# Single-bank evictions for batch 0: mix units that leave PSUM by two engines side by side, and turns and last DFTs that rotate over all eight banks

## The chip, the cores and the metric

The kernel runs on one core of a Trainium2 chip. The metric is the device time of one execution in microseconds (us). The kernel before takes 849.84 us (median of three executions, 849.62 to 851.12). One trace per kernel was taken by the hardware profiler. Engines are named as in the profile: PE is TensorE (matmuls), DVE is VectorE, ACT is ScalarE, POOL is GpSimd, SP issues transfers. PSUM, where matmuls write, is used here as eight banks of 512 float32 columns for each of 128 partitions; the pools below take them all.

## The reference

A frequency-domain mixer is followed by a feed-forward layer. Cut to what matters:

```python
# x: 8 batches x 3008 positions x 256 channels, float32
X = np.fft.rfft(x, axis=1)
Yr = Xr @ w_r - Xi @ w_i + b_r          # 256 x 256, complex
Yi = Xr @ w_i + Xi @ w_r + b_i
Yr = np.sign(Yr) * np.maximum(np.abs(Yr) - 0.01, 0.0)      # likewise Yi
y = np.fft.irfft(Yr + 1j * Yi, n=3008, axis=1)
# feed-forward on 24064 tokens, hidden width 2048
g = s * np.maximum(y @ w_in, 0.0) ** 2 + b
out = g @ w_out
```

## The kernel before

The transforms of length 3008 = 94 x 32 are done as matmuls. Batch 0 runs alone at the front, as nothing is there yet to lie beside it; the batches 1 to 7 are mixed into the feed-forward matmuls of the batch before, and there PE is full. Only batch 0 is changed. Its path, in six *units* for each half of the output channels (`ec`):

first DFT -> `mix` (96 matmuls) -> copy g out of PSUM -> `fwd_dft` -> soft threshold (Relu on ACT into m, then z on DVE) -> `inv_dft` -> copy vt -> `turn` (a transpose by the identity) -> copy vs -> `last_dft` -> copy yt -> feed-forward.

The bias must be added once. DVE adds it while it copies g; ACT here only copies, so where it does, a *seed* matmul puts the bias into the bank of the forward DFT first.

```python
hpool = ...tile_pool(name="psh", bufs=2, PSUM)   # two tiles of two banks
apool = ...tile_pool(name="psa", bufs=2, PSUM)   # two single banks
fpool = ...tile_pool(name="psf", bufs=2, PSUM)   # two single banks
def evac(dst, src, cols): ...   # ACT or DVE, whichever has the lower sum of estimates

def mix(ec, u):
    ps = two_banks().rearrange("p h (j r e) -> p (h j) r e", j=2, r=2)
    for j in range(4):
        ...                                   # 2 matmuls of 256 columns for each j
    g = vpool.tile([P, 4, 2, P], F16, ...)
    if u % 3 == 1:
        nc.scalar.copy(out=g, in_=ps)         # 1,024 columns, bias by a seed
    else:
        nc.vector.tensor_tensor(out=g, in0=ps, in1=b_g[...], op=ALU.add)

def fwd_dft(ec, u):
    seeded = u % 3 == 1
    if seeded:
        nc.tensor.matmul(ps, sel_t, b_h[...], start=True, stop=False, ...)
    for j in range(4):
        ...                                   # 2 matmuls of 128 columns for each j
    # Relu on ACT, then z on DVE

def turn(ec, k):
    ps = two_banks()
    ...                                       # 8 matmuls
    evac(vs[...], ps[0:96]..., 1024)

def last_dft(ec, n2):
    ps = [one_bank(), other_bank()]
    ...                                       # 8 matmuls, two evac of 384

# the loop over the twelve units
    mix(*steps[i]); fwd_dft(*steps[i - 1]); inv_dft(*steps[i - 2])
    k = i - U - 2
    if 0 <= k < 4:
        turn(0, k)
    if 0 <= k - 1 < 4:
        last_dft(0, 8 * (k - 1))
    if i >= 2 * U:
        some(3)                               # three pieces of batch 1's first DFT
# then, for the second half: turn(1, k), some(1), last_dft(1, 8 * (k - 1))
```

## Time and profile before

| | before |
|---|---|
| span of the trace | 847.2 us |
| PE busy | 833.7 us, 98% |
| DVE, ACT busy | 691.5 us, 641.2 us |
| first mix starts | 13.72 us |
| batch 1's first forward DFT starts | 64.58 us |

What the change takes apart is seen in the groups by shape, here of the kernel before between 13.7 and 50 us. A row has the line, engine, operation and tiles, output and input shape, the count, then the busy time in us and the mean ns of one, then the idle time before them with what ended it:

```profile
L419 DVE TENSOR_TENSOR g<-psh,b_g 128x1024 f16<-128x1024 f32 x8 | 9.7, 1217 | 0.6 <-PE psh L409 0.5
...
L171 ACT CAST vs<-psh 96x1024 f16<-96x1024 f32 x6 | 6.1, 1012 | 0.7 <-PE psh L473 0.6
L416 ACT CAST g<-psh 128x1024 f16<-128x1024 f32 x4 | 4.1, 1014 | 0.1
L175 DVE CAST vs<-psh 96x1024 f16<-96x1024 f32 x2 | 2.4, 1215 | 0.2 <-PE psh L473 0.2
```

All twelve copies g and all eight copies vs are of 1,024 columns, and take 1.0 us on ACT or 1.2 on DVE. Whatever else is queued on that engine stands behind such a copy, and both of the tile's banks stay taken until it is done.

### The profile page before, as it was taken

How to read it: one execution, taken by the hardware profiler on the slowest of the kernel's cores; microseconds unless marked ns; L12 is line 12 of the kernel's file. 1: busy time of each engine (PE TensorE's matmuls, PEld its weight loads, DVE VectorE, ACT ScalarE, POOL GpSimd, SP SyncE). 2: the span in 40 equal slices, each digit the busy share in tenths (PEclk: the TensorE clock that was granted, in tenths of full speed). 3: DMA queues.
4: the chain of work that ended last, by engine and by line, in shares of the span. 5: the costliest groups of instructions: out<-in, count | busy, mean ns of one | idle time of the engine just before them, and what ended most of it. 6: DMA issues, size and time to landing. Idle time of an engine off the chain costs nothing.

```text
span 847.2 us, 17072 instructions
## 1 busy us (share of the span) xinstructions
PE 833.7 (98%) x6645; PEld 598.8 (71%) x6645; DVE 691.5 (82%) x1016; ACT 641.2 (76%) x854; POOL 45.6 (5%) x71
## 2 busy tenths in 40 slices
PE   7999999999999999999999999999999999999997
PEld 6757767777677766777677776777667777766765
DVE  5899987888878987888878888798977888776674
ACT  5888877787778877787777887787877777766673
POOL 4331000000000000000000000000000000000000
PEclk9999999999999999999999999999999999999999
DMA  8946467224762367324762248613354223411111
GB/s 200 173 131 139 118 160 192 78 70 108 193 161 60 99 157 191 95 79 108 179 173 57 73 105 202 170 41 91 101 156 120 61 79 98 112 33 39 38 44 50
DMA packets 105746, 96.06 MB, mean 113 GB/s; under 512 B 9542, under 2 KB 97482, under 8 KB 104322
## 3 DMA queue, kind: packets, MB, share of 16 engines
q1 hardware_dynamic: 99218, 80.55, 32.9%
q0 software_dynamic: 6448, 14.42, 10.5%
q8 instruction: 52, 0.85, 0.4%
q14 instruction: 28, 0.23, 0.1%
HBM read 53.52 MB, written 46.66 MB: 118 GB/s over the span
## 4 chain that ended last, share of the span: by engine, by line
PE 87%; DVE 4%; ACT 3%; DMA 3%; issue 2%; SPq 0%; POOL 0%; DVEq 0%; ACTq 0%; POOLq 0%
PE psa L819 36%; PE psh L748 35%; PE psf L614 4%; PE psf L549 2%; PE psf L600 2%; PE psf L585 2%; PE psf L644 2%; PE psf L697 2%; ACT rt L755 1%; DVE gt L762 1%; DMA out_dram<-ost 1%; DMA x<-in_x_dram 1%; DMA us<-ud 1%; DMA F_c<-dft_fwd 1%; PE psh L409 1%
## 5 line engine op out<-in xcount | busy, mean ns | idle before, releaser
L755 ACT ACTIVATE rt<-psh 128x1024 f32<-128x1024 f32 (+2 forms) x384 | 386.9, 1009 | 119.3 <-PE psh L748 117.9
L762 DVE TENSOR_TENSOR gt<-rt 128x1024 f16<-128x1024 f32 (+2 forms) x321 | 384.1, 1200 | 97.9 <-ACT rt L755 97.2
L819 PE MATMUL psa<-w_out_t,gt 128*128 128x256 f16 (+1 forms) x3024 | 454.3, 272 | 0.1
L819 PEld LDWEIGHTS <-gt 128*128 128x128 f16 (+1 forms) x3024 | 301.0, 101 | 187.2 <-issue 1.7
L748 PE MATMUL psh<-yt,w_in 128*128 128x512 f16 (+1 forms) x1344 | 396.7, 378 | 0.3 <-ACT rt L755 0.3
L748 PEld LDWEIGHTS <-w_in 128*128 128x128 f16 x1536 | 142.9, 98 | 27.4 <-issue 2.1
L829 DVE SCALAR_TENSOR_TENSOR ost<-psa,s_bc,bias_bc 128x512 f32<-128x512 f32 (+2 forms) x97 | 71.1, 733 | 8.3 <-PE psa L819 7.1
L759 ACT ACTIVATE gt<-rt 128x1024 f16<-128x1024 f32 (+2 forms) x63 | 66.2, 1051 | 1.0
L619 DVE TENSOR_TENSOR ring<-psf,s 128x512 f16<-128x512 f32 x84 | 57.6, 685 | 3.7 <-PE psf L614 3.1
L171 ACT CAST v<-psf 128x512 f16<-128x512 f32 x78 | 45.2, 581 | 18.8 <-PE psf L644 18.8
L171 ACT CAST xf<-psf 128x512 f16<-128x512 f32 x82 | 47.9, 585 | 10.9 <-PE psf L585 10.9
L171 ACT CAST u<-psf 96x512 f16<-96x512 f32 x77 | 44.6, 580 | 11.0 <-PE psf L549 10.7
L748 PE MATMUL psh<-tail,w_in 128*128 128x512 f16 (+1 forms) x192 | 52.1, 353 | 0.0
L614 PE MATMUL psf<-W_g,xf 128*128 128x256 f16 x336 | 50.4, 273 | 0.0
L171 ACT CAST yt<-psf 128x480 f16<-128x480 f32 (+2 forms) x75 | 38.1, 521 | 13.6 <-PE psf L697 13.6
L200 POOL DMA_DIRECT2D x<-in_x_dram x36 | 18.7, 526 | 429.7 <-PE psf L549 428.6
L549 PE MATMUL psf<-x,A_t 94*96 94x512 f16 x104 | 39.7, 381 | 1.7 <-ACT yt L171 0.5
L625 DVE TENSOR_TENSOR ring<-ring,high 128x512 f16<-128x512 f16 x84 | 35.5, 423 | 2.3
L626 DVE TENSOR_TENSOR ring<-ring 128x512 f16<-128x512 f16 x84 | 35.5, 423 | 1.9
L624 DVE TENSOR_TENSOR ring<-ring,low 128x512 f16<-128x512 f16 x84 | 35.4, 422 | 1.6
L614 PEld LDWEIGHTS <-xf 128*128 128x128 f16 x336 | 32.9, 98 | 3.8
L697 PE MATMUL psf<-C_t,vs 96*128 96x96 f16 x448 | 33.0, 205 | 0.1
(88 smaller groups left out, 489.4 us busy)
## 6 DMA issues: line engine op xcount, KB each, us to landing
out_dram<-ost SPq DMA_DIRECT2D x152, 128.0 KB
ud<-u SPq DMA_DIRECT2D x28, 384.0 KB
us<-ud SPq DMA_DIRECT2D x28, 384.0 KB
vd<-v SPq DMA_DIRECT2D x42, 256.0 KB
vs<-vd SPq DMA_DIRECT2D x14, 768.0 KB
x<-in_x_dram POOLq DMA_DIRECT2D x28, 376.0 KB, 6.8
ring<-ring SPq DMA_DIRECT2D x280, 32.0 KB
out_dram<-ost SPq DMA_DIRECT2D x16, 120.0 KB
```

Of the source, the lines that this page charges most:

```text
L171: return None, nc.scalar.copy(out=dst, in_=src)
L549: nc.tensor.matmul(ps[0:96, :], A_t[0:N1, :], x16[(b, c)][0:N1, j * D : (j + 2) * D], start=True, stop=True,)
L614: nc.tensor.matmul(ps[:, r, :], xt[:, 2 - r, dc], W_g[:, dc, r], start=(dc == 0), stop=(dc == DC - 1),)
L619: nc.vector.tensor_tensor(out=t, in0=ps, in1=hold[i // 2][:, i % 2].unsqueeze(1).to_broadcast([P, 2, D]), op=ALU.add,)
L625: nc.vector.tensor_tensor(out=m, in0=m, in1=high, op=ALU.min)
L697: nc.tensor.matmul(ps[:, j * 96 : (j + 1) * 96], vs[(b, h)][:, k, ec * P : (ec + 1) * P], C_t, start=True, stop=True,)
L748: nc.tensor.matmul(o, w_in_t[dc][:, mc * P : (mc + 1) * P], r, start=(dc == 0), stop=(dc == DC - 1),)
L755: nc.scalar.activation(out=rt[:, :, 0:w], in_=ps[:, :, 0:w], func=AF.Relu)
L759: nc.scalar.activation(out=gt[:, :, 0:w], in_=rt[:, :, 0:w], func=AF.Square)
L762: nc.vector.tensor_tensor(out=gt[:, :, 0:w], in0=rt[:, :, 0:w], in1=rt[:, :, 0:w], op=ALU.mult)
L819: nc.tensor.matmul(ps[0:size, h, :], gts[(ti, mc // 2)][:, mc % 2, sub * size : (sub + 1) * size], w_out_t[:, mc, :], start=(mc == 0), sto ...
L829: nc.vector.scalar_tensor_tensor(out=ost[0:size, 0:k], in0=ps[0:size, 0:k], scalar=s_bc[0:size], in1=bias_bc[0:size, 0:k], op0=ALU.mult, o ...
```

## The change

The intent: while batch 0 runs, the four banks of `psh` are a pool of single banks, `psm`. A mix unit fills two of them; DVE empties one half and ACT the other, side by side. Turns are cut in halves as well. Turns, last DFTs and batch 1's first DFT take a bank from all eight in rotation, and the last DFTs of the first half are moved behind the forward DFT of the last unit. The pool `psm` is closed after batch 0, and `psh` opens in its place.

```diff
+    def any_bank():
+        turn_of[0] += 1
+        if "h" in pools:
+            return (other_bank, one_bank)[turn_of[0] % 2]()
+        return (mix_bank, one_bank, mix_bank, other_bank)[turn_of[0] % 4]()
... in mix
-            ps = two_banks().rearrange("p h (j r e) -> p (h j) r e", j=2, r=2)
+            for half in range(2):
+                ps = mix_bank().rearrange("p (j r e) -> p j r e", j=2, r=2)
...
-            if u % 3 == 1:
-                nc.scalar.copy(out=g, in_=ps)
+                if half:
+                    nc.scalar.copy(out=g[:, 2:4], in_=ps)
+                else:
+                    nc.vector.tensor_tensor(out=g[:, 0:2], in0=ps, in1=b_g..., op=ALU.add)
... in fwd_dft: every unit is seeded, for its second half alone
-            if seeded:
-                nc.tensor.matmul(ps, sel_t, b_h...[P, 4, P] ...)
+                if j == 2:
+                    nc.tensor.matmul(ps[:, 2:4], sel_t, b_h...[P, 2, P] ...)
... in turn
-            ps = two_banks()
-            for j in range(8):
+            for i in range(2):
+                ps = any_bank() if ec else mix_bank()
+                for j in range(4):
... in last_dft
+            if ec or n2 >= 16:
+                ps = [any_bank(), any_bank()]
+            else:
+                ps = [one_bank(), other_bank()]
... in the loop
-            if 0 <= k - 1 < 4:
-                last_dft(0, 8 * (k - 1))
+            for n in {1: (0,), 2: (8,), 4: (16, 24)}.get(k, ()):
+                last_dft(0, n)
... in batch 1's first DFT
-            ps = other_bank() if more_banks and i % 2 else one_bank()
+            ps = any_bank() if more_banks else one_bank()
... at the end of the program's front
-    more = first_batch()
+    with tc.tile_pool(name="psm", bufs=4, space=PSUM) as pool:
+        pools["m"] = pool
+        more = first_batch()
+    pools["h"] = ctx.enter_context(tc.tile_pool(name="psh", bufs=2, space=PSUM))
```

More of the change, by code (lines that the diff above doesn't have):

```diff
@@ L145 @@
     bigpool = ctx.enter_context(tc.tile_pool(name="big", bufs=1))
-    hpool = ctx.enter_context(tc.tile_pool(name="psh", bufs=2, space=bass.MemoryType.PSUM))
     apool = ctx.enter_context(tc.tile_pool(name="psa", bufs=2, space=bass.MemoryType.PSUM))
@@ L176, in evac, with mix_bank @@
         return nc.vector.tensor_scalar_mul(out=dst, in0=src, scalar1=scale), None
+    pools = {}
+    def mix_bank():
+        return pools["m"].tile([P, 512], F32, name="psm", tag="psm")
+    turn_of = [0]
+    def any_bank():
[3 more added lines that the diff above has]
+        return (mix_bank, one_bank, mix_bank, other_bank)[turn_of[0] % 4]()
     def two_banks():
-        return hpool.tile([P, 2, 512], F32, name="psh", tag="psh")
+        return pools["h"].tile([P, 2, 512], F32, name="psh", tag="psh")
     def one_bank():
@@ L356, in first_batch @@
             for dc in range(DC):
-                ps = one_bank() if dc else two_banks()[:, 0]
+                ps = one_bank() if dc else mix_bank()
                 with tc.issue_after(last_pe.ins):
@@ L404, in mix @@
         def mix(ec, u):
-            ps = two_banks().rearrange("p h (j r e) -> p (h j) r e", j=2, r=2)
-            for j in range(4):
-                q = 4 * u + j
-                for dc in range(DC):
-                    nc.tensor.matmul(
-                        ps[:, j], ut[:, dc, 4 * q : 4 * q + 4, :],
-                        W_t[:, dc, :, ec * P : (ec + 1) * P],
-                        start=(dc == 0), stop=(dc == DC - 1),
-                    )
-            g = vpool.tile([P, 4, 2, P], F16, name="g0", tag="v")
-            if u % 3 == 1:
-                nc.scalar.copy(out=g, in_=ps)
-                load["act"] += 1.02
-            else:
-                nc.vector.tensor_tensor(
-                    out=g, in0=ps,
-                    in1=b_g[:, :, ec * P : (ec + 1) * P].unsqueeze(1).to_broadcast([P, 4, 2, P]),
-                    op=ALU.add,
-                )
-                load["dve"] += 1.2
-            gs[(ec, u)] = g
+            g = vpool.tile([P, 4, 2, P], F16, name="g0", tag="v")
+            gs[(ec, u)] = g
+            for half in range(2):
+                ps = mix_bank().rearrange("p (j r e) -> p j r e", j=2, r=2)
+                for j in range(2):
+                    q = 4 * u + 2 * half + j
+                    for dc in range(DC):
+                        nc.tensor.matmul(
+                            ps[:, j], ut[:, dc, 4 * q : 4 * q + 4, :],
+                            W_t[:, dc, :, ec * P : (ec + 1) * P],
+                            start=(dc == 0), stop=(dc == DC - 1),
+                        )
+                if half:
+                    nc.scalar.copy(out=g[:, 2:4], in_=ps)
+                    load["act"] += 0.58
+                else:
+                    nc.vector.tensor_tensor(
+                        out=g[:, 0:2], in0=ps,
+                        in1=b_g[:, :, ec * P : (ec + 1) * P].unsqueeze(1).to_broadcast(
+                            [P, 2, 2, P]
+                        ),
+                        op=ALU.add,
+                    )
+                    load["dve"] += 0.69
         def fwd_dft(ec, u):
@@ L429, in fwd_dft @@
             g = gs.pop((ec, u))
-            seeded = u % 3 == 1
-            if seeded:
-                nc.tensor.matmul(
-                    ps, sel_t,
-                    b_h[:, ec * P : (ec + 1) * P].unsqueeze(1).to_broadcast([P, 4, P]),
-                    start=True, stop=False, skip_group_check=True,
-                )
             for j in range(4):
                 q = 4 * u + j
+                if j == 2:
+                    nc.tensor.matmul(
+                        ps[:, 2:4], sel_t,
+                        b_h[:, ec * P : (ec + 1) * P].unsqueeze(1).to_broadcast([P, 2, P]),
+                        start=True, stop=False, skip_group_check=True,
+                    )
                 for r, f in enumerate((F_t[:, q, :], F_2[q // H][:, q % H, :])):
                     nc.tensor.matmul(
-                        ps[:, j, :], f, g[:, j, r, :], start=(r == 0 and not seeded),
-                        stop=(r == 1), skip_group_check=seeded,
+                        ps[:, j, :], f, g[:, j, r, :], start=(r == 0 and j < 2),
+                        stop=(r == 1), skip_group_check=True,
                     )
@@ L470, in turn @@
         def turn(ec, k):
-            ps = two_banks()
-            for j in range(8):
-                nc.tensor.matmul(
-                    ps[0:96, j // 4, (j % 4) * P : (j % 4) * P + P],
-                    vt[:, ec, 8 * k + j, :], eye_t, start=True, stop=True,
-                )
-            h, n = divmod(8 * k, HW)
-            evac(
-                vs[(0, h)][:, n : n + 8, ec * P : (ec + 1) * P],
-                ps[0:96].rearrange("p h (j e) -> p (h j) e", e=P), 1024,
-            )
+            for i in range(2):
+                ps = any_bank() if ec else mix_bank()
+                n = 8 * k + 4 * i
+                for j in range(4):
+                    nc.tensor.matmul(
+                        ps[0:96, j * P : j * P + P], vt[:, ec, n + j, :], eye_t,
+                        start=True, stop=True,
+                    )
+                h, n = divmod(n, HW)
+                evac(
+                    vs[(0, h)][:, n : n + 4, ec * P : (ec + 1) * P],
+                    ps[0:96].rearrange("p (j e) -> p j e", e=P), 512,
+                )
         yt = yts[0] = ypool.tile([P, DC, N2, 96], F16, name="yt", tag="yt")
         def last_dft(ec, n2):
-            ps = [one_bank(), other_bank()]
+            if ec or n2 >= 16:
+                ps = [any_bank(), any_bank()]
+            else:
+                ps = [one_bank(), other_bank()]
             for j in range(8):
@@ L844, in schedule @@
             plan.setdefault(start + (i * span) // len(units), []).append(u)
-    more = first_batch()
+    with tc.tile_pool(name="psm", bufs=4, space=bass.MemoryType.PSUM) as pool:
+        pools["m"] = pool
+        more = first_batch()
+    pools["h"] = ctx.enter_context(
+        tc.tile_pool(name="psh", bufs=2, space=bass.MemoryType.PSUM)
+    )
     load.update(act=0.0, dve=0.0)
```

## The prediction

> **What bounds the kernel now.** I read the page's busy slices first, then the windows of the first 58 us, then the waits of TensorE, then its timeline. TensorE (PE) is busy 98% of the span, and the slices show where the rest is:
>
> ```profile
> PE   7999999999999999999999999999999999999997
> ```
>
> Only the first and the last slice (21 us each) fall below nine tenths. The change touches batch 0 alone, which is the front of the program, so the windows there matter:
>
> ```profile
> core 0: us, PE busy (x) PEld busy (x) DVE busy (x) ACT busy (x) POOL busy (x), PEclk, DMA share, GB/s
> ...
> 13.70:35.00 21.30, 19.68 (x238) 16.84 (x239) 15.97 (x24) 16.96 (x25) 8.70 (x13) 1.00 0.95 215
> 35.00:42.00 7.00, 5.54 (x74) 4.38 (x72) 6.54 (x10) 5.80 (x12) 1.75 (x3) 1.00 0.91 126
> 42.00:50.00 8.00, 7.13 (x84) 4.80 (x82) 7.07 (x12) 6.96 (x13) 7.50 (x7) 1.00 0.34 100
> 50.00:58.00 8.00, 7.71 (x38) 3.62 (x37) 7.20 (x8) 8.00 (x12) 0.73 (x1) 1.00 0.33 98
> ```
>
> From 35 us on VectorE (DVE) and ScalarE (ACT) are nearly full while PE has holes: the emptying of PSUM bounds it. From 50 to 58 ACT has no idle time at all. Before 35 PE looks full, but a matmul's record is longer than its place in the queue, so I count starts instead. In the timeline:
>
> ```profile
> 16.77 0.22 PE L440 MATMUL psf<-g,F_t 128*128 128x128 f16 x1 [1.09 <-DVE g L419]
> 16.82 0.22 PE L440 MATMUL psf<-g,F 128*128 128x128 f16 x1
> ...
> 17.21 1.04 PE L409 MATMUL psh<-W_t,ut 128*128 128x256 f16 x8
> 18.08 0.38 PE L432 MATMUL psf<-b_h,sel_t 128*128 128x512 f16 x1
> 18.30 0.22 PE L440 MATMUL psf<-g,F_t 128*128 128x128 f16 x1
> ```
>
> The start-to-start times are 0.055 us for a matmul of 128 columns, 0.109 for 256 (0.87 for eight), 0.216 for 512 (18.08 to 18.30), and likewise 0.042 for 96. The same reading of the DVE and ACT timelines gives their pitch: DVE 1.13 us for 1,024 columns of PSUM, 0.60 for 512, 0.46 for 384; ACT 0.91, 0.48 and 0.38, with 0.58 for the Relu of 512.
>
> Work of PE from 13.72 (first mix) to 61.53, the point from which the instruction order of the two kernels is identical to the end: 96 mix matmuls x 0.109 = 10.4; 96 forward x 0.055 = 5.3; 4 seeds 0.9; 48 inverse 2.7; 64 turns 3.5; 64 last DFTs 2.7; 16 of batch 1's first DFT x 0.216 = 3.5; 42 of the first feed-forward matmul 9.1; 16 of the second 1.7; bias 0.1. Sum 39.9 of 47.8 us. So 7.9 us is all that could be won, under 1% of 849.84; after 61.5 PE is dense (119.63 busy of 120 from 80 to 200).
>
> **What the Trainium skill says.** "Perfetto Trace Analysis", section "Optimizing Scalar/DVE Operations", gives about 125 ns per-instruction overhead for DVE on PSUM and 51 ns for Scalar on PSUM, and says that where they cause bubbles on other engines, "breaking up instructions may allow work to be completed sooner". The trace: two halves cost 2 x 0.60 - 1.13 = 0.07 us more on DVE and 2 x 0.48 - 0.91 = 0.05 on ACT, so DVE pays less here than the page says. The same page, "Matmul Optimizations", asks that all 8 PSUM banks be used; before, the turns use only the two double tiles (psh), the last DFTs only psf and psa. "TensorE: Matmul & The Clock Gate", section "Wait — 56ns, not 53.3ns?", gives 55.6 and 215.7 ns start to start at 128 and 512 columns; the trace agrees.
>
> **The change, part by part.**
> Mix. Before, 8 of 12 units leave by DVE (8 x 1.13) and 4 by ACT (4 x 0.91), 12.7 us. After, 12 x 0.60 on DVE and 12 x 0.48 on ACT, 13.0: DVE loses 1.8, ACT gains 2.1, so the automatic balance sends more later copies to DVE. PE gets 12 seeds of 256 columns for 4 of 512: 12 x 0.109 - 4 x 0.216 = +0.45 us.
> Turns. 8 x 1,024 columns become 16 x 512: about 8.6 instead of 7.7 us, half on each engine.
>
> I laid the new instruction order out by hand with these pitches, 0.20 us from a matmul group's end to its reader, 0.06 from a copy's end (start plus duration, 0.69 DVE, 0.58 ACT) to PE.
>
> (a) First forward DFT. PE waits 1.09 us for g. The DVE half now ends at 16.15 instead of 16.71, but the ACT half can start only when ACT has placed F_t (16.24) and ends at 16.85, so the second half of the forward group starts at 16.9. Its end moves from 17.21 to 17.1: gain 0.1.
>
> (b) Steady steps. PE per step: mix 0.87 + forward 0.44 + seed 0.11 + inverse 0.22 = 1.64. Before, mix 2 to mix 8 took 17.21 to 27.60, 1.73 per step, because each z queued behind a 1.13 us copy. After, the inverse needs z, which comes 0.20 + 0.69 + 0.03 + 0.69 + 0.06 = 1.7 us after its forward group, while PE has 1.64 of other work: some 0.03 to 0.1 lost per step. Forward group 7 ends at 28.8 instead of 29.36: gain 0.5 in all.
>
> (c) The turns begin. Before, mix 9 waits 0.28 for the double tile behind the turn; after, it does not. Step 10 lies about 1.0 earlier.
>
> (d) The end of the mixes. Before, forward 11 waits for z and inverse 11 comes only after batch 1's DFTs, themselves waiting:
>
> ```profile
> 39.02 0.22 PE L440 MATMUL psf<-g,F_t 128*128 128x128 f16 x1 [0.65 <-DVE z L447]
> ...
> 40.64 0.38 PE L549 MATMUL psa<-x,A_t 94*96 94x512 f16 x1 [0.44 <-DVE vt L175]
> ...
> 43.28 0.38 PE L549 MATMUL psa<-x,A_t 94*96 94x512 f16 x1 [0.31 <-DVE vt L175]
> 43.50 1.06 PE L473 MATMUL psh<-eye_t,vt 128*96 128x128 f16 x16
> ```
>
> After, forward 11 goes before the last DFTs (37.2) and the DFTs take any free bank; the last vt is out at 41.1 and the second half's turns start at 41.2 instead of 43.5. Gain 2.1 to 2.3 here.
>
> (e) The tail. Both evicting engines are full: 9 copies u, 8 vs (512 columns) and 8 yt (384) at a joint rate of 1/0.60 + 1/0.48 = 3.75 and 1/0.46 + 1/0.38 = 4.8 per us is 4.5 + 1.7 = 6.2 us, ending at 47.4 plus small waits. The feed-forward tiles (psh) now take over the banks of batch 0 and cannot be interleaved with the last DFTs as before (first one at 47.45); PE reaches them at 47.6, and ACT's first rt is at 48.65 instead of 49.97. Then 1 copy u is left instead of 4 (3 of them on ACT, about 1 us).
>
> (f) To the common order ACT bounds: nine rt x 0.95, one u 0.5, two bias copies 0.4 each after 48.65: 58.6, the common matmul at 59.0 instead of 61.3. VectorE's squares run back to back from 49.7 and are 2.0 earlier.
>
> Sum of what each part adds: (a) 0.1, (b) 0.4 more, (c) 0.5 more, (d) 1.2 more, and (e) and (f) hold it at 61.3 - 59.0, about 2.2 us, with the 0.45 us of seeds already inside. All of it lies on PE's path, as PE is dense afterwards. I take 2.1: 847.7 us.
>
> **The rivals.**
> *The gain is given back at the hand-over.* The psh tiles wait for the last batch 0 copy, PE and ACT start the feed-forward cold. For: the pool of four banks closes before they open. Against: by (e) the last of those copies is out at about the same 47.5. If each of the last copies slips by half a microsecond the gain is 1 us: 848.8.
> *ACT becomes the bound in the steps.* It gets 2.1 us more, and its Relu must wait behind a g half. Per step ACT has 0.48 + 0.58 + 0.48 = 1.54 with every vt on it, under PE's 1.64, so only queueing hurts; if each of twelve steps lost 0.15, 1.8 us go, and the time is about 849.5.
> *A transfer holds it.* GpSimd's w_sum, behind the load of w_out (landed at 41.4), is ready at 50.8, and PE meets it after sixteen feed-forward matmuls, by my layout at 51.6. That is a floor 0.8 us below: 847 at best. Other loads (w_in, x of batch 1) land ten microseconds before use.
> *Better packing than by hand.* If PE's holes shrank to 4 us, 846.5, less the floor just named.
>
> **Range and chances.** The ceiling of 7.9 us and the worst rival, a full undoing with the seeds on top (850.5), lie well within 2% (17 us). The three runs before spread over 1.5 us. Range 846.4 to 849.3; faster by over 2% 0.01, within 2% 0.98, slower 0.01.
>
> **What would show it.** DVE's g at 0.69 us and ACT's at 0.58, x12 each; no wait of a mix on g; the second half's first turn near 41.2; the first rt near 48.7; w_sum's matmul without a wait; PE unchanged after 61.5. Wrong if the chain from Relu to z to inverse stalls PE by more than 0.1 per step (then step b), if the first rt comes later than 49.5 (step e), or if the time won at 60 us is lost again to a wait in the body, which I see no sign of.

## The result, and the profile after

The changed kernel takes 847.79 us (median of four executions, 847.55 to 848.22) beside 849.73 for the kernel before in the same rounds (849.23 to 851.12). The ratio is 0.9975, with a 95% interval of 0.9958 to 0.9992. The change is worth about 2 us, 0.2%: within 2%, and 0.1 us from the predicted 847.7. The trace's span went from 847.16 to 846.25 us, 0.9 only; why the trace moved less than the time is settled below.

The row of PE's busy slices after:

```profile
PE   8999999999999999999999999999999999999997
```

The first slice went from 7 to 8, and the rest of the row is as it was. The same windows after; columns are the stretch and its length, then busy time and count for each engine, the granted clock of PE, the share of the DMA engines, and GB/s:

```profile
13.70:35.00 21.30, 20.77 (x265) 18.25 (x263) 17.79 (x32) 19.40 (x35) 9.12 (x13) 1.00 0.99 219
35.00:42.00 7.00, 6.35 (x82) 5.02 (x80) 7.00 (x13) 6.44 (x15) 1.71 (x3) 1.00 0.94 134
42.00:50.00 8.00, 6.92 (x72) 4.33 (x70) 6.40 (x12) 7.07 (x14) 7.45 (x8) 1.00 0.41 116
50.00:58.00 8.00, 7.79 (x40) 3.77 (x39) 7.80 (x7) 7.80 (x12) 0.39 (x1) 1.00 0.51 156
```

PE's busy time over the four windows rose from 40.06 to 41.83 us of 44.30. In the first two windows PE and both evicting engines do more. In the last, DVE is now as full as ACT (7.80 each), where before ACT stood at 8.00 and DVE at 7.20; this turns out to matter.

The groups by shape after, in the same stretch as shown of before:

```profile
L435 DVE TENSOR_TENSOR g<-psm,b_g 128x512 f16<-128x512 f32 x12 | 8.1, 682 | 1.2 <-PE psm L426 1.0
...
L432 ACT CAST g<-psm 128x512 f16<-128x512 f32 x12 | 7.0, 588 | 1.2 <-PE psm L426 0.9
...
L170 ACT CAST vs<-psm 96x512 f16<-96x512 f32 x8 | 4.6, 590 | 0.5 <-PE psm L491 0.5
...
L450 PE MATMUL psf<-b_h,sel_t 128*128 128x256 f16 x12 | 3.3, 272 | 0.0
```

Twelve halves on each engine, at 682 and 588 ns, and twelve seeds. Now PE's timeline after: start, duration, operation, and in brackets how long PE was idle before it and who ended that:

```profile
16.44 0.23 PE L456 MATMUL psf<-g,F_t 128*128 128x128 f16 x1 [0.31 <-ACT F_t L325]
...
17.27 1.04 PE L426 MATMUL psm<-W_t,ut 128*128 128x256 f16 x8
...
36.84 0.22 PE L456 MATMUL psf<-g,F_t 128*128 128x128 f16 x1
...
41.26 0.42 PE L491 MATMUL psa<-eye_t,vt 128*96 128x128 f16 x4 [0.22 <-DVE vt L174]
...
45.39 0.34 PE L511 MATMUL psf<-C_t,vs 96*128 96x96 f16 x4 [0.28 <-ACT vs L170]
46.25 0.59 PE L570 MATMUL psa<-x,A_t 94*96 94x512 f16 x2 [0.52 <-ACT yt L170]
...
47.73 0.38 PE L570 MATMUL psf<-x,A_t 94*96 94x512 f16 x1 [0.28 <-ACT u L170]
47.94 1.89 PE L769 MATMUL psh<-yt,w_in 128*128 128x512 f16 x8
```

The wait of 1.09 us for g is now 0.31 for the table F_t. Forward group 11 starts at 36.84 without a wait, where before it came at 39.02 after 0.65. The second half's turns start at 41.26, not 43.50. Then, on the last copies of batch 0, PE waits 0.28 + 0.52 + 0.28 = 1.08 us, and the first feed-forward matmul comes at 47.94.

To compare traces whose loads landed at different moments, I count from the end of forward group 0 (17.21 us in the trace before, 17.27 after). Counted so, the two or three traces of a kernel agree within about 0.02 us up to the first rt, ACT's first feed-forward activation:

| us after forward group 0 | before | predicted | after | gain: predicted, measured |
|---|---|---|---|---|
| forward group 7 ends | 12.15 | 11.7 | 11.67 | 0.45, 0.48 |
| forward group 9 ends | 17.20 | | 16.46 | about 0.9, 0.74 |
| first turn of the second half | 26.30 | 24.1 | 23.99 | 2.2, 2.31 |
| first feed-forward matmul | 30.25 | 30.5 | 30.67 | -0.25, -0.42 |
| first rt | 32.77 | 31.55 | 31.88 | 1.22, 0.89 |
| batch 1's first forward DFT | 47.38 | | 45.70 | 2.2, 1.68 |

The last row is past the point from which both kernels have the same order, 61.32 and 59.70 us in the traces.

How does the tail go from 0.89 at the first rt to 1.68? DVE's timeline has it, the squares of the feed-forward. Before:

```profile
51.03 1.23 DVE L762 TENSOR_TENSOR gt<-rt 128x1024 f16<-128x1024 f32 x1 [0.80 <-ACT rt L755]
52.17 0.68 DVE L175 CAST u<-psa 96x512 f16<-96x512 f32 x1
52.78 10.31 DVE L762 TENSOR_TENSOR gt<-rt 128x1024 f16<-128x1024 f32 x9
```

After:

```profile
50.20 11.49 DVE L783 TENSOR_TENSOR gt<-rt 128x1024 f16<-128x1024 f32 x10 [1.18 <-ACT rt L776]
```

DVE has no gap in its first ten squares in either kernel, and batch 1's DFT keeps a fixed distance from them. In ten of the eleven traces of changed kernels (after, and e1 to e5, e7, e9 to e11 below) it starts 1.27 to 1.29 us after the end of the tenth square, and in the eleventh, e8, and the three of before 1.47 to 1.50. The link is the eighth square: PE's first matmul that reads it starts 0.06 us after its end in all fourteen traces. From there PE's order is full, 3.49 us to the DFT, and 3.70 in before and e8, where one more feed-forward matmul (0.216 us) stands between. In the trace after, and in e1, where the squares were delayed by 0.49 us:

```profile
59.47 0.39 PE L840 MATMUL psa<-w_out_t,gt 128*128 128x256 f16 x2
```

```profile
60.32 0.39 PE L840 MATMUL psa<-w_out_t,gt 128*128 128x256 f16 x2 [0.35 <-DVE gt L783]
```

So the squares are the last to come, but in the undisturbed trace by a hair: PE shows no wait on gt there, and counted by starts it stood some 0.02 us before that matmul. Its waits from the first feed-forward matmul on are on ACT's rt (0.17 and 0.04 us). PE, fed by ACT, and DVE arrive together; only where a square was held up, in e1, e2, e5, e8 and e10, does PE wait for gt, 0.20 to 0.49 us.

The copy u between the first two squares before is gone, since only one copy u, on ACT, is left after the first rt. So the gain at this point is 0.89 for the earlier first square, 0.57 for the shorter run of ten (51.03 to 63.09 is 12.06; now 11.49), and 0.22 for the one matmul less behind the squares: 1.68.

From there to the end the trace of before took 782.58 us and that of after 783.29. The difference is, to 0.05 us, one wait in the middle of the program, from PE's timeline after:

```profile
130.88 0.60 PE L718 MATMUL psf<-C_t,vs 96*128 96x96 f16 x10 [0.76 <-DMA vs<-vd]
```

Batch 1's last DFT waits for its input to come back from DRAM. So the trace shows -1.68 + 0.71, and 0.06 for the start, a net of -0.9 us.

### The profile page after: what moved, and what is told of

Read it like the earlier page. It is cut to its first block, busy times and chain, and to the rows that moved or that the text cites. A ratio compares the mean times of both kernels' runs of the same rounds, so it can differ in the third digit from the quotient of the medians.

```text
span 846.2 us, 17115 instructions
## 1 busy us (share of the span) xinstructions
PE 833.9 (99%) x6653; PEld 599.6 (71%) x6653; DVE 691.8 (82%) x1026; ACT 642.7 (76%) x864; POOL 46.0 (5%) x71
## 4 chain that ended last, share of the span: by engine, by line
PE 89%; DVE 4%; DMA 3%; ACT 3%; issue 1%; POOL 0%; DVEq 0%; ACTq 0%; SPq 0%; POOLq 0%
PE psa L840 36%; PE psh L769 36%; PE psf L635 4%; PE psf L570 2%; PE psf L621 2%; PE psf L606 2%; PE psf L718 2%; PE psf L665 2%; ACT rt L776 1%; DVE gt L783 1%; DMA vd<-v 1%; PE psm L426 1%; DMA vs<-vd 1%; DMA x<-in_x_dram 1%; DMA F_c<-dft_fwd 0%
## 5 line engine op out<-in xcount | busy, mean ns | idle before, releaser
L170 ACT CAST v<-psf 128x512 f16<-128x512 f32 x78 | 45.3, 582 | 18.7 <-PE psf L665 18.7
```

The source lines that it names most:

```text
L170: return None, nc.scalar.copy(out=dst, in_=src)
```

## The experiments

The theory at the outset: the split with two engines side by side does the steps, order and rotation do the end of the mixes, and what is missing at the end comes from the tail. Twelve kernels ran; unless said otherwise their results were correct. All marks are counted as in the table above; the column "to the end" is the time from batch 1's first forward DFT to the end of the trace.

| | median us | fwd 7 | fwd 9 | turn | first rt | first square | tenth ends | batch 1's DFT | to the end |
|---|---|---|---|---|---|---|---|---|---|
| before | 849.73 | 12.15 | 17.20 | 26.30 | 32.77 | 33.82 | 45.88 | 47.38 | 782.6 |
| after | 847.79 | 11.67 | 16.46 | 23.99 | 31.88 | 32.93 | 44.42 | 45.70 | 783.3 |
| e1 change again | 848.55 | 11.67 | 16.46 | 23.99 | 31.88 | 32.93 | 44.91 | 46.19 | 782.8 |
| e2 split only | 849.17 | 11.67 | 16.46 | 24.64 | 31.82 | 32.88 | 45.89 | 47.16 | 783.0 |
| e3 one engine | 848.73 | 11.35 | 15.85 | 24.55 | 32.40 | 33.44 | 44.92 | 46.20 | 782.8 |
| e4 old order | 848.66 | 11.67 | 16.46 | 24.24 | 32.13 | 33.18 | 44.66 | 45.95 | 783.8 |
| e5 no seeds | 847.83 | 11.03 | 15.67 | 23.17 | 31.06 | 32.12 | 44.42 | 45.70 | 782.6 |
| e7 both engines at the end only | 848.58 | 11.35 | 16.09 | 23.68 | 31.53 | 32.58 | 44.05 | 45.33 | 784.3 |
| e8 early hand-over | 848.04 | 11.66 | 16.46 | 23.99 | 30.70 | 31.76 | 44.28 | 45.75 | 783.0 |
| e9 three edits | 847.47 | 11.74 | 16.59 | 24.10 | 32.01 | 33.06 | 44.54 | 45.83 | 782.3 |
| e10 last DFT later | 847.83 | 11.67 | 16.46 | 23.98 | 31.87 | 32.94 | 44.78 | 46.05 | 782.6 |
| e11 change again | 847.81 | 11.66 | 16.46 | 23.98 | 31.88 | 32.94 | 44.42 | 45.69 | 782.7 |

The times do not rank e1 to e4: the interval of each against before includes 1. The argument rests on the marks, of one trace each. In both repeats of before (e6, e12) the marks are those of before within 0.03 us.

**e1: the change once more, five rounds.** No edit.

> The changed kernel unedited. Is the 0.8 us wait of the last DFT of batch 1 (PE psf on the load vs<-vd, near 131 us) part of the change or a chance of that one execution? If it belongs to the change, this profile shows 0.5 to 1.0 us of it again and the kernel of before shows none. If it is chance, it is mostly gone (under 0.3 us) and the span after the first common matmul comes back to 785.9 us, so the profiled gain rises from 1.0 to about 1.6 to 2.1 us. The ratio should stay at 0.9975, about 2.1 us, with the front accounting for 1.6 to 2.2.

Measured: 848.55 us (847.71 to 849.41), ratio 0.9988 (0.9976 to 1.0001). The marks up to the first rt are those of the first trace to 0.01 us, and the wait on vs<-vd is not there. But batch 1's DFT comes 0.49 later, and the timelines of DVE and POOL say why:

```profile
50.56 11.98 DVE L783 TENSOR_TENSOR gt<-rt 128x1024 f16<-128x1024 f32 x10 [1.18 <-ACT rt L776]
```

```profile
50.57 1.80 POOL L345 TENSOR_TENSOR w_sum<-acc 128x256 f16<-128x256 f32 x1
```

GpSimd's last addition for w_sum took 1.80 us beside the squares; in the first trace it started at 49.67, before them, and took 0.72. One square took 1.75 us instead of 1.21, and the ten 11.98 instead of 11.49. GpSimd's sums begin when w_out has landed, so where the last of them falls is a matter of that load. So the profiled gain did not rise to the 1.6 to 2.1 us that I expected: the span is 0.58 us shorter than before's (1.19 won at batch 1's DFT, 0.42 lost ahead of forward group 0, 0.19 lost after). A second difference is the granted clock; the window of 8 to 12 us in e1, then in e11, the same program:

```profile
8.00:12.00 4.00, 3.87 (x48) 3.51 (x46) 1.95 (x5) 2.73 (x6) 1.77 (x2) 0.60 1.11 200
```

```profile
8.00:12.00 4.00, 3.19 (x53) 2.51 (x54) 2.28 (x6) 2.86 (x6) 1.21 (x1) 1.00 1.10 203
```

PE ran at a granted 0.60 in the first DFT of batch 0, before the mixes, in matmuls of which the change moved only the bank that they write. This fell on 5 of the 14 traces (e1, e3, e4, e5, e7) and on none of the three of before, and not on the other two of the change; whether the change has a part in it stays open. The mixes start between 13.72 and 15.62 us over all traces, and between 13.72 and 14.60 in those of before alone.

**e2: the split of the mix alone.** Turns, last DFTs, order and batch 1's banks as before, in the new pools.

```diff
-                ps = any_bank() if ec else mix_bank()
+                ps = mix_bank()
-            if ec or n2 >= 16:
-                ps = [any_bank(), any_bank()]
-            else:
-                ps = [one_bank(), other_bank()]
+            ps = [one_bank(), other_bank()]
-            for n in {1: (0,), 2: (8,), 4: (16, 24)}.get(k, ()):
-                last_dft(0, n)
+            if 0 <= k - 1 < 4:
+                last_dft(0, 8 * (k - 1))
-            ps = any_bank() if more_banks else one_bank()
+            ps = other_bank() if more_banks and i % 2 else one_bank()
```

> The mix leaves by both engines from four banks, but turns, last DFTs and batch 1's first DFT keep the banks and the order of before. My theory (the sum of the prediction): only steps a to c remain, 0.5 to 1.0 us, so 848.7 to 849.2 against 849.7. The rival that the side-by-side exit makes the gain: 847.6 to 848.1, as the full change. A second rival, that the split alone only costs (0.45 us of seeds, smaller copies): 849.9 to 850.4.

Measured: 849.17 us, ratio 0.9995 (0.9982 to 1.0007). In the trace the split alone, with the halved turns that come with single banks, gives all of the gain at forward groups 7 and 9 and 1.66 of the 2.31 us at the turns. At the first rt it is even with the change (31.82 and 31.88). What order and rotation win at the turns is thus gone by the first rt. Their worth would have to lie in the copies u that are done by then; here one copy is again between DVE's squares. This trace can't weigh that well: w_out landed late, and the addition of w_sum, at 52.88, took 1.59 us among the squares; the ten squares with that copy took 13.01 us. Of the 1.52 more than after, the copy is some 0.55 and the meeting with GpSimd some 0.96 (two squares took 3.32 instead of 2.36).

**e3: halves, but each unit by one engine in turn**, as before the change (one unit in three by ACT), so with four seeds of 512 columns again.

```diff
-                if half:
-                    nc.scalar.copy(out=g[:, 2:4], in_=ps)
+                if u % 3 == 1:
+                    nc.scalar.copy(out=g[:, 2 * half : 2 * half + 2], in_=ps)
... the same half in DVE's branch, and in fwd_dft
-                if j == 2:
+                if j == 0 and seeded:          # 512 columns instead of 256
```

> All banks and the order of the change, but both halves of a mix unit leave by one engine in turn, as before two units in three by VectorE and one by ScalarE (and the seeds as before, 0.45 us less PE work). My theory: the side-by-side exit is worth step b, about 0.4 us, against which the seeds stand, so 847.8 to 848.4. The rival that the side-by-side exit makes the gain: 849.2 to 849.8. The rival that the exit does not matter at all: 847.3, the seeds' 0.45 us below the change.

Measured: 848.73 us, ratio 0.9990 (0.9978 to 1.0003). My theory, that the steps gain because the two engines work side by side, falls: without that, forward group 7 is 0.32 us earlier than in the change and group 9 0.61 earlier. Emptying single banks by halves does it; whether it is the shorter copy or the bank that comes free sooner no run separates. The seeds explain part of what the second engine costs there: up to group 7 the change has 7 x 0.109 = 0.76 us of them and e3 3 x 0.216 = 0.65, up to group 9 0.98 and 0.65, so 0.11 of the 0.32 and 0.33 of the 0.61; the rest the runs do not divide. Side by side pays only at the end of the mixes: from forward group 9 to the turns e3 takes 8.70 us, the change 7.53. At the first rt e3 is 0.52 behind.

**e4: only the old order of the last DFTs.** The rotation stays.

```diff
-            for n in {1: (0,), 2: (8,), 4: (16, 24)}.get(k, ()):
-                last_dft(0, n)
+            if 0 <= k - 1 < 4:
+                last_dft(0, 8 * (k - 1))
```

> The change with one thing undone: the last DFTs of the first half are issued one per step after their turn, as before, not two held back behind the last mixes. My theory has this order in step d (forward 11 ahead of the last DFTs): 0.3 to 0.7 us are lost, 848.1 to 848.5, and forward 11 or its neighbours wait 0.3 us or more for z near 37 to 39 us. The rival that the eight banks alone do it: 847.6 to 847.9, no such wait.

Measured: 848.66 us, ratio 0.9989 (0.9975 to 1.0003). The loss is 0.25 us, at the turns, the first rt and batch 1's DFT alike, below what I expected, and the wait is another one than I named. PE's timeline of e4:

```profile
38.71 0.22 PE L456 MATMUL psf<-g,F_t 128*128 128x128 f16 x1 [0.61 <-ACT yt L170]
```

Forward group 11 waits for a psf bank that a last DFT holds until ACT has copied yt, and not for z. So the moved lines are worth a quarter of a microsecond by themselves. Its trace has the wait on vs<-vd too, 1.0 us.

**e5: no seeds.** The halves by ACT then lack the bias, a wrong result; the bias is so small that the comparison still passed.

```diff
-                if j == 2:
-                    nc.tensor.matmul(ps[:, 2:4], sel_t, b_h...[P, 2, P], start=True, ...)
-                        ps[:, j, :], f, g[:, j, r, :], start=(r == 0 and j < 2),
+                        ps[:, j, :], f, g[:, j, r, :], start=(r == 0),
```

> Wrong result on purpose: the twelve seed matmuls (the bias of the halves that leave by ScalarE) are left out, 12 x 0.109 = 1.31 us of TensorE work. Times in the trace are counted from the end of forward group 0, which repeated to 0.01 us between two runs of the change (forward 7 at 11.67, forward 9 at 16.46, first turn of the second half at 23.99, first rt at 31.88). My theory: the steps are then held by the chain Relu, z, inverse (1.70 us against 1.53 of other PE work) and the tail by eviction, so only a part comes out: forward 7 at 11.1 to 11.5, first rt at 31.3 to 31.7. The rival that the seeds are wholly on the path: forward 7 at 10.9, first rt at 30.6 to 30.8.

Measured: 847.83 us. Twelve seeds are 12 x 0.109 = 1.31 us of PE; leaving them out brings the first rt 0.82 us forward and batch 1's DFT not at all (45.70 in both). Group 7 at 11.03 and the first rt at 31.06 are earlier than I expected and later than the rival had them. The waits of PE in e5 have two that the change lacks; columns are what waited, on what, us in total, times, longest:

```profile
PE psa L834 <- DVE gt L777: 0.5, 1, 0.5
...
PE psa L349 <- POOL w_sum L345: 0.2, 1, 0.2
```

The squares start 0.81 us earlier and meet GpSimd's addition (1.59 us), and the ten take 12.30 instead of 11.49. In this trace the prediction's third rival is at work, through DVE: GpSimd's sums after the load of w_out take back what the front had won.

**e6: the kernel before again**, one look, no edit.

> The kernel of before, for a second trace. Is the late first mix of the changed kernels (14.2 to 15.6 us, against 13.72 in the one trace of before) of their making? If it is chance (loads of x, and in three of five executions half the granted clock in the first 8 to 16 us), this trace may show it too, with a first mix anywhere from 13.7 to 15.6, and the offsets from forward group 0 repeat: first turn of the second half 26.3, first rt 32.8, batch 1's first forward DFT 47.4, all within 0.3. If the four single banks cause it, the first mix is at 13.7 again with full clock.

Measured: 849.48 us; marks as in the first trace (first rt 32.75), no wait on vs<-vd.

**e7: both engines only where e3 lost**, units 9 to 11; the others by one engine in turn.

```diff
-                if half:
+                if (half if ec and u > 2 else u % 3 == 1):
... and in fwd_dft the seed covers what ACT copied
+            lo = 2 if ec and u > 2 else 0 if u % 3 == 1 else 4
```

> Units 0 to 8 leave in two halves by one engine in turn (VectorE, ScalarE, VectorE), only the last three by both side by side. With one engine throughout, forward 9 was 0.61 us earlier than in the change (15.85 against 16.46: fewer seeds, no wait on two engines), but it lost 1.17 between forward 9 and the first turn of the second half, where VectorE was late with the two halves of unit 11. If that reading is right: forward 9 at 15.9 and the first turn of the second half at 23.3 to 23.6 instead of 23.99, first rt at 31.2 to 31.5. Rival, that the backlog of VectorE and ScalarE decides and not the side-by-side exit of the last units: first turn at 24.0 to 24.5, first rt no earlier than 31.9.

Measured: 848.58 us. The direction is right and a little short: group 9 at 16.09, turns at 23.68, first rt at 31.53, batch 1's DFT at 45.33, the earliest of all. GpSimd's last addition was over before the squares here (48.66 to 49.38 us), and the 0.35 us won at the first rt are all there at the DFT (0.37). The end gives it back:

```profile
131.00 0.60 PE L719 MATMUL psf<-C_t,vs 96*128 96x96 f16 x10 [1.51 <-DMA vs<-vd]
```

**e8: an earlier hand-over of the banks.** The pool of batch 0 is closed and `psh` opened after the third turn of the second half.

```diff
+            if k == 2:
+                yield
-        return more
+        yield more
-        more = first_batch()
+        batch = first_batch()
+        next(batch)
... and after psh is opened
+    more = next(batch)
```

> The change with an earlier hand-over: the pool of batch 0's four banks closes before the last 2 calls of last DFTs and the last turn, so that the feed-forward tiles can start among them as in the kernel before. Step e of the prediction put the cost of the hand-over at nothing; the trace of the change shows VectorE idle 0.61 us, ScalarE 0.52 and 0.42, and VectorE 1.18 before its first square. If these are the cost of the hand-over, batch 1's first forward DFT comes 0.5 to 1.0 us earlier than the 45.70 (46.19 in the repeat) of the change, at 44.9 to 45.5. Rival, that the total of eviction fixes the end whatever the order: 45.6 to 46.3.

Measured: 848.04 us. The first feed-forward matmul comes 2.76 us earlier than after the change and the first rt 1.18 earlier, but batch 1's DFT does not (45.75). DVE's timeline of e8:

```profile
49.05 1.70 DVE L785 TENSOR_TENSOR gt<-rt 128x1024 f16<-128x1024 f32 x1 [0.69 <-ACT rt L778]
50.67 0.68 DVE L174 CAST u<-psa 96x512 f16<-96x512 f32 x1
51.28 10.29 DVE L785 TENSOR_TENSOR gt<-rt 128x1024 f16<-128x1024 f32 x9
```

The first square meets GpSimd's additions (1.70 us instead of 1.21), a copy u is again between the squares, and the tenth ends only 0.14 us earlier than after. So the earlier hand-over wins nothing at the end of this one trace. Why is not separated: the meeting cost 0.46 us (12.52 for the ten squares, against 12.06 with a copy u in before), and without it, by that difference as an estimate, the DFT would have come near 45.3. That the hand-over costs nothing is thus not shown.

**e9: three edits together**, as a try at something better: both engines for units 0 and 9 to 11 only, half of the placing of F_t by GpSimd, and batch 1's last DFT two slots later, so as to miss the wait on vs<-vd. Five rounds.

```diff
-                if half:
+                if (half if (u > 2 if ec else u == 0) else u % 3 == 1):
-            nc.scalar.copy(out=blocks(F_t)[r, 0:H, :, a], in_=F_c[r])
+            if a:
+                nc.gpsimd.tensor_copy(out=blocks(F_t)[r, 0:H, :, a], in_=F_c[r])
+            else:
+                nc.scalar.copy(out=blocks(F_t)[r, 0:H, :, a], in_=F_c[r])
... and the seeds in fwd_dft as in e7
-    schedule(mark[1] - 14, 12, s4_units(1))
+    schedule(mark[1] - 12, 12, s4_units(1))
```

> A candidate that should beat both: units 0 and 9 to 11 by both engines, the others in halves by one engine in turn (its seeds are fewer); GpSimd instead of ScalarE places half of F_t; batch 1's last DFTs start two slots later, so that the load vs<-vd is in before they are met. From forward group 0's end, first rt at 31.2 to 31.6 (change 31.88); forward group 0 ends 0.2 to 0.4 us sooner after F_c than the 2.55 of the change if GpSimd takes under 1.4 us; no wait on vs<-vd. In the same rounds 0.5 to 1.3 us faster than the change. Rival: GpSimd's copy takes over 2 us and forward 0 waits for it, so nothing is gained there; the eviction and w_sum floor hold the rest, within 0.3 us of the change.

Measured: 847.47 us (847.30 to 847.78), ratio 0.9973 (0.9959 to 0.9986), the fastest of all by 0.3 us; but its front is not ahead of the change's (first rt 32.01). The copy by GpSimd won nothing: it took 0.89 us, and a copy of DVE beside it 0.87, which takes 0.25 in the trace after:

```profile
14.74 0.87 DVE L337 COPY F<-F_c 64x384 f16<-64x384 f16 x1
```

From the start of the first placing of F_t to the end of forward group 0 it took 2.84 us instead of 2.55.

**e10: the change with batch 1's last DFT two slots later**, the last edit of e9 alone. Five rounds on the same chip.

> The change with one schedule edit: the last DFTs of batch 1 begin two slots (four feed-forward matmuls and about as many of the second) later. If the give-back of 0.5 to 1.6 us after the front is the wait on vs<-vd, that wait is gone or under 0.2 us and the time from batch 1's first forward DFT to the end is 782.5 to 782.9, in all five rounds 0.3 to 0.8 us faster than the change in the mean. Rival, that the later start pushes yt against the first tile of batch 1: a new wait on yt of 0.3 us or more and no gain.

Measured: 847.83 us (847.53 to 848.16), ratio 0.9977 (0.9964 to 0.9989), no wait on vs<-vd in its trace. GpSimd's addition ended at 50.72, after the first square's start at 50.18, and the ten squares took 11.84.

**e11 and e12: the change and the kernel before, five rounds each**, beside e9 and e10. No edits.

> The change once more, as the yardstick of these rounds and as a third trace: offsets of the front repeat to 0.05 us (first rt 31.88); ratio to before between 0.9970 and 0.9990. The wait on vs<-vd is there in one of two traces so far: chance says it may be absent or up to 1 us.

> The kernel before as one of the kernels, for a third trace and five more times on this chip: ratio 0.9990 to 1.0010, no wait on vs<-vd (0 of 2 so far) if that wait belongs to the changed front, or one in about half the traces if it is chance; half the granted clock at 8 to 12 us (0 of 2 so far, 5 of 9 in changed kernels) likewise.

Measured: the change 847.81 us (847.50 to 849.04), ratio 0.9980 (0.9968 to 0.9993); before 849.72 (849.36 to 850.54), ratio 1.0 (0.9988 to 1.0013). The text for e12 miscounts by one: the half clock had been seen in 5 of 8 traces of changed kernels then, and none of before's had it. Neither e11 nor e12 has it, nor the wait. Their spans differ by 1.9 us, 845.9 and 847.8, as do their medians. This pair is the cleanest comparison, and settles why the first pair of traces showed only 0.9: the one traced run of the change there had the wait on vs<-vd.

The mean times of e9, e10 and e11 in these rounds are 847.49, 847.81 and 848.13 us. The change's own five runs spread over 1.5 us, so no version is shown to beat it.

## Why the prediction was right, point by point

The time, 847.79 us for a predicted 847.7, came out by the mechanism told. The gain of (d) was credited to the wrong edits, and the end of (e) and the last leg of (f) were mis-sized. That the first session's median fell within 0.1 us of the prediction is luck in part: the parts in the trace sum to 1.68 us, and the sessions gave 1.0 to 2.1.

**What bounds the kernel.** Right: only the front could be shortened. PE's work there did not shrink, and the holes in the four windows went from 4.24 us to 2.47.

**(a) First forward DFT.** Right: 0.08 us from the first placing of F_t, for 0.1, and held, as said, by F_t (the 0.31 us wait).

**(b) Steady steps.** Right in size: 0.48 us for 0.45, at 11.67 / 7 = 1.67 us a step. No mix waits on g. The reason given, that each z queued behind a copy of 1.13 us, agrees with e3: halves on one engine keep the gain and add 0.32. The second engine does not help there.

**(c) The turns begin.** Right in direction, a little too large: 0.74 us in all for about 0.9 to 1.0.

**(d) The end of the mixes.** Right: 2.31 us for 2.1 to 2.3. By e2 the split has 1.66 of it and order and rotation together 0.65, by e4 the order alone 0.25. The prediction put what (d) adds to (c), 1.2 us, down to the order and the free banks. Measured it is 2.31 - 0.74 = 1.57, and 1.66 - 0.74 = 0.92 of that comes with the split: the sum was right, its parts were not.

**(e) The tail, mis-sized.** The prediction had "small waits" and the first rt at 48.65; PE's three waits there sum to 1.08 us, and the first rt is 0.33 late on the common count. Its other claim, that the hand-over is not what holds it, stays open: e8 found no gain from an earlier one, but in a trace that GpSimd's addition disturbed.

**(f) To the common order: right up to its last leg.** "ACT bounds" fits most of the way. ACT in the trace after:

```profile
55.83 1.94 ACT L776 ACTIVATE rt<-psh 128x1024 f32<-128x1024 f32 x2
57.97 1.02 ACT L776 ACTIVATE rt<-psh 128x1024 f32<-128x1024 f32 x1 [0.20 <-PE psh L769]
```

ACT has no idle time from 50.97 to 57.77 us, and from the start of the first rt to the end of the ninth it took 9.85 us (49.14 to 58.99), just what the prediction's terms sum to (48.65 to 58.5; it wrote 58.6). What failed is the last leg. From the end of the ninth rt to the common matmul 0.71 us passed (59.70) for the 0.5 that its terms leave, because the path does not run through that rt: ACT itself waits for PE before it, and the last input to come is DVE's eighth square, with PE as late within some 0.02 us. The prediction had the squares back to back and 2.0 us earlier than before; they were 1.40 earlier (the tenth ends at 61.69 for 63.09), mostly as the first began at 50.20 and not 49.7. And they were on the path: where GpSimd's addition meets them, the run of ten is longer by 0.35 to 0.96 us and PE waits for gt. The gain after the first rt was to be 0.98; it was 0.79. Together with the 0.33 of (e), that is the difference of the 2.2 predicted and the 1.68 measured.

**The rivals.** An earlier hand-over won nothing (e8), which leaves its cost open. The prediction's "full undoing with the seeds on top" sums to 850.3 (849.84 + 0.45) and not 850.5. ACT did not become the bound of the steps. The floor set by w_sum is real, but mostly does not look as the prediction drew it: PE's wait for w_sum is 0.2 us in e5, and the larger part is the slower squares beside GpSimd's addition. Only in e2, where w_out landed late, did PE stand 0.76 us before w_sum's matmul, until w_sum and a copy u behind the slowed square both ended at 54.5 us. In the change itself it appears by chance, in e1 (0.49 us) and not in the first trace or e11.

**What would show it wrong.** The prediction saw "no sign of" a wait in the body. There is one, before batch 1's last DFT: in 1 of 3 traces of the change, in 5 of 11 traces of all its variants (two of these, e9 and e10, move the reader away), in none of 3 of before. Where it is 0.76 us or more, 7.5 to 7.7 us pass from the issue of the last write of vd to that of the read into vs; where it is 0.23 to 0.24 (e2, e8), 7.2 to 7.7; in the traces without it 5.4 to 6.5. For a given program it is chance. Whether an earlier front makes it likelier stays open; three traces of before are too few, and e10, which moves the reader away, gained no more than noise.

**The scatter.** Over the three sessions the mean gain was 2.1, 1.0 and 1.7 us. The change's runs of the second session lie higher without a change of code; the record has another chip for e1 to e4 than for e9 to e12. GpSimd's meeting with the squares and the lower granted clock were both seen in the trace e1 of that session, and may be why; runs without a trace can't be asked.

## What to carry to other kernels

When an eviction of two banks holds up the matmuls, cut it into single banks first and see what that gives: here halves on one engine gave all of the gain of the steady steps, and the second engine with its extra bias matmuls paid only where one engine had fallen behind. Follow the path to the point from which the order is the same, and ask of each input there which comes last: here TensorE, fed by ScalarE, and VectorE's eighth square came together. When GpSimd's addition fell among the squares, 0.8 and 1.2 us won at the first rt were gone at that point (e5, e8); e7, which it missed, kept its 0.35. For differences of a few tenths of a per cent take several traces of the same program and count from a common event, since a load that lands half a microsecond later moves everything behind it.

## What the Trainium skill lacked or had wrong

- "Perfetto Trace Analysis", section "Optimizing Scalar/DVE Operations": its overhead of about 125 ns for DVE on PSUM is more than a split costs here. Two halves of 512 columns against one of 1,024 cost 0.07 us more on DVE start to start, and 0.05 on ACT, where its 51 ns agrees. Its advice to break up instructions, which it gives for engines that are not saturated, held where DVE and ACT were busy 15.97 and 16.96 of 21.30 us, in the steps: in e3 halves on one engine alone kept all of the steps' gain (0.32 us ahead of the version with two).
- The same section warns that GpSimd and DVE share an SBUF read port, and "SBUF — State Buffer", section "SBUF: two separate sides", says that this pair is an exclusive lock, so that the loser blocks wholly. The traces agree, and I had left it out of the prediction: a copy of DVE took 0.87 us instead of 0.25, until GpSimd's had ended (e9), and GpSimd's addition took 1.59 to 1.80 us instead of 0.72 where a square had started first. The second page names such a square too, a DVE operation with two SBUF inputs against GpSimd. What the runs add is the price: one small addition of GpSimd made a run of ten squares longer by 0.49 us in e1 and 0.81 in e5.
- "TensorE: Matmul & The Clock Gate", section "HAM oscillation — how this bites in real kernels", gives as the abstract rule no gaps of PE over about 3.4 us. Keeping to that was not enough here, and the rule alone does not explain it: in e1 the granted clock fell to 0.60 in 8 to 12 us, and the longest single wait of PE that the trace lists is 1.4 us, for a load; 5 of 14 traces fell to 0.51 to 0.61 in that stretch. What set it off there the runs do not tell.
